# Two weight loads, the first reads of the way back and one first-stage result change queue and place, with four more filler matmuls

## The chip, the cores and the metric

The kernel runs on one core of one Trainium2 chip. The metric is the device time of one execution in microseconds, the median of several runs. The core has a matrix engine (PE, with its weight loads shown as PEld), a vector engine (DVE), an activation engine (ACT), a general engine (POOL) and a sync engine (SP). Each engine works through its own list of instructions in order. SP, ACT and POOL can also issue DMA transfers; a transfer that has to wait for something holds up all that stands behind it on the engine that issues it.

## The reference

```python
def _attn_ref(x, filt_r, filt_i):            # x: (8, 3008, 256)
    X = np.fft.rfft(x, axis=1)
    F = (filt_r + 1j * filt_i)[None, :, :]   # (1505, 256)
    y = np.fft.irfft(X * F, n=x.shape[1], axis=1)
    return y.astype(np.float32)

def _moe_ref(x, w_in, w_out):                # x: (24064, 256)
    h = x @ w_in                             # w_in: (256, 2048)
    g = h - np.tanh(h)
    return (g @ w_out).astype(np.float32)    # w_out: (2048, 256)
```

The first function filters eight sequences in the frequency domain, and the second is fed with its result, batch after batch, as 24064 rows. `x` and the filters come as float32. The two weight matrices come as 64-bit floats (their random values are scaled by a 64-bit factor), and the kernel converts them to 32 bits itself, with integer operations on their words.

## The kernel before, in words

The length 3008 is split as 64 x 47, so that each transform becomes two stages of matrix products. The first stage (`first`) multiplies the samples by a 64-point matrix for each of 47 residues; these are taken in pairs, which leaves 24 groups of rows. Its results are written to memory (`ct1`), read again in another order, taken through the 47-point stage (`forth`), multiplied by the filter (`filtered`) and taken back through the 47-point stage (`back`). The result goes to memory once more (`ct2`). The last stage (`last`, with the tile `e2` read from `ct2`) makes the rows `ut`, on which the two weight matrices work: `up` multiplies by `w_in`, `shrink` computes h - tanh(h) from a chain of activations, `down` multiplies by `w_out`. In most of the run `up` and `down` take seven products for eight, with seven planes of each weight matrix (`wu` and `wd`): planes 0, 1, 3 and 6 are converted weights, and planes 2, 4, 5 (and a new 6) are sums of them, made late by `sums`. For the first four units (`up_plain`, `down_plain`) only the four converted planes are used.

The first batch is handled in a prologue of its own, before any weight product runs. In it the 32 columns of the 47-point stage are cut in seven slots (`SLOTS`, six with five columns and one with two; `last_g` is 6). A loop over the slots `g` (L1264 to L1302) runs `forth`, `filtered` and the product back (`back0`, and `back` for the last slot), and `way_back()` (L1255) issues the product back of the slot that is next in line. `back0` writes its result to `ct2` through POOL's queue for the slots 0 to 2, SP's for 3 and 4, and ACT's for 5 (L1150). `back` for the last slot copies with ACT (L481) and writes each copy in two halves, one through ACT's queue and one through SP's (L483).

At the end of the prologue `rest(a, n, queues)` (L1130) reads the rows `a` to `a + n` of each of four groups from `ct2` into `e2`, in four DMAs (L1134): first the rows of the slots 0 to 4, as soon as they are written, and, after the last `way_back()`, the remaining seven. PE's first product of the main part (L595, in `last`) needs all of `e2`. Between these, `first(2, ...)` issues its first five loads from SP, `convert(100)` finishes the conversion of the first five pieces of weights, `first1` makes the first-stage results of the second batch that were not yet made (four matmul pairs, L1232, four ACT copies, L1238, and four writes to `ct1`, L1239), and `warmer(n)` issues `n` matmuls whose result nobody reads (L1086).

The weights come in 16 jobs of 512 KB. `begun` (L240) issues a job's raw load and returns a generator that then converts it in steps: an ACT activation (L181), five DVE operations (L183 to L194) and one or two DVE additions into `wu` or `wd` (L201). The first five jobs are converted in the prologue. The others go through `tiles1` (L1043), whose raw buffers are the halves of the tiles `ft` (two jobs), `a2` (two jobs), `ft` and so on, and whose working buffers are the halves of the tile `xy`, in turn. `buffer(tag)` (L278) gives the halves of a tile alternately. `weights` (L247) converts jobs 5 to 15 step by step in the first units of the main part, so that the place of each step in the engines' lists is fixed when the program is built, and issues the loads of the later jobs on POOL's queue.

The whole program is emitted with an order written out by hand: each engine executes in the order of the source, and only waits for data and buffers are put in automatically.

The lines that matter here: the loads of the jobs 7 and 8 (counted from 0) in the loop, L1281; the two calls of `rest`, L1303 and L1305; `convert(100)` and `first1`, L1308 and L1309; `warmer(8)`, L1314; the copies and writes of `first1`, L1234 to L1240.

Of the kernel before, what the change touches and what calls it, by code (L numbers as in the profile page):

```python
# [9 lines left out]
F32 = mybir.dt.float32  # L10
# [7 lines left out]
BATCH, SEQ, DM = 8, 3008, 256  # L18
NQ, NR = 64, 47
NA = NQ // 2  # L20
NH = (NR + 1) // 2
SG = 5
# [95 lines left out]
def kernel(  # L118
# [9 lines left out]
    nc = tc.nc  # L128
    V, G, ACT = nc.vector, nc.gpsimd, nc.scalar
    f_d, both_d, g_d, whole_d, mats_d, one_d, wide_d, pairs_d, whole_pairs_d, split_d = (  # L130
        nc.inline_tensor(v, name=n).ap()
        for v, n in zip(_consts(), ("f", "f_both", "g", "g_whole", "mats", "one", "wide",
                                    "g_pairs", "g_whole_pairs", "f_split")))

    ct1 = [nc.dram_tensor(f"ct1_{b}", (4 * NA * NH, DM), F32, kind="Internal")
           for b in range(1, BATCH)]
# [9 lines left out]
    def dram(t, off, dims):  # L146
        return bass.AP(tensor=t, offset=off, ap=[list(d) for d in dims])
# [20 lines left out]
    wu = cst.tile([128, 7, DFF // 2], F32, name="wu")  # L168
# [57 lines left out]
    def sums(u, n=4):  # L226

        w = (wu if u < 4 else wd)[:, :, 256 * (u % 4):256 * (u % 4) + 256]
        V.tensor_add(w[:, 4], w[:, 6], w[:, 3])
        yield  # L230
        for to, one_in, less in ((5, 4, 0), (2, 1, 5), (6, 0, 6))[:n - 1]:
            V.tensor_sub(w[:, to], w[:, one_in], w[:, less])
            yield
# [6 lines left out]
    def begun(tiles, job, queue=nc.sync):  # L240
        j = converted(tiles, *job, queue)
        next(j)
        return j
# [3 lines left out]
    def weights(tiles, jobs, queue, began, ahead, after=()):  # L247

        began += [begun(tiles, job, queue) for job in jobs[len(began):ahead]]
        yield  # L250
        for k in range(len(jobs)):
            pending[0] = len(jobs) - k
            for n, _ in enumerate(began[k]):
                yield
                if (after or k > 2) and n == 2 and k + 1 < len(jobs):
                    next(began[k + 1])
            if k + ahead < len(jobs):
                began.append(begun(tiles, jobs[k + ahead], queue))
            pending[0] = len(jobs) - k - 1
            for u in dict(after).get(k, ()):  # L260
                yield from sums(u)
# [16 lines left out]
    def buffer(tag):  # L278

        turns[tag] = 1 - turns.get(tag, 1)  # L280
        return kept[tag][:, turns[tag]]
# [755 lines left out]
    with tc.tile_pool(name="tr", bufs=2) as tr, tc.manual_schedule():  # L1037
# [16 lines left out]
        with tc.tile_pool(name="pro", bufs=1) as pro, \  # L1054
                tc.tile_pool(name="ps0", bufs=8, space=bass.MemoryType.PSUM) as ps0:

            def z0(name, shape):
                return ps0.tile(shape, F32, tag="z", bufs=8, name=name)
# [3 lines left out]
            def big(shape, dtype, name):  # L1062

                return pro.tile(shape, dtype, tag="big", bufs=3, name=name)
# [16 lines left out]
            def warmer(n, t=None):  # L1081

                warm = z0("warm", [128, 256])
                t = f0[:, 0:2].rearrange("p a n -> p (a n)") if t is None else t
                for _ in range(n):
                    nc.tensor.matmul(warm, t[:, 0:128], t, start=True, stop=True)  # L1086
# [43 lines left out]
            def rest(a, n, queues):  # L1130

                e2 = e2s[0][0]
                for j in range(4):
                    queues[j % len(queues)].dma_start(  # L1134
                        e2[NA * j + a:NA * j + a + n],
                        dram(ct2[0], (NA * j + a) * NH * DM, [[NH * DM, n], [1, CH * DM]]))
# [16 lines left out]
            last_g = len(SLOTS) - 1  # L1153
# [17 lines left out]
            jobs = parts_of((0, 1, 2, 4, 3, 5, 6, 7))  # L1171
# [5 lines left out]
            for c in range(3):  # L1177
# [14 lines left out]
                r = 8 * c  # L1192
# [27 lines left out]
            def convert(n):  # L1220

                for _ in range(n):
                    next(early, None)
# [3 lines left out]
            def first1(x1):  # L1227

                for r in range(0, 8, 2):
                    pf = z0("pf", [128, 2, DM])  # L1230
                    for k in range(2):
                        nc.tensor.matmul(pf[:, k], f0[:, r + k], x1[:, r + k],  # L1232
                                         start=True, stop=True)
                    if r % 4 == 0:  # L1234
                        two = (tr.tile([128, 2, 2, DM], F32, tag="a1", bufs=1, name="a1") if r else
                               buffer("xy").rearrange("p (m n) c -> p m n c", m=2))
                    a1 = two[:, r // 2 % 2]
                    ACT.copy(a1, pf)  # L1238
                    nc.sync.dma_start(  # L1239
                        dram(ct1[1], r * DM, [[NH * DM, 128], [1, 2 * DM]]), a1)  # L1240
                    yield

            a2 = {0: across(0)}
            convert(5)
# [19 lines left out]
            for g in range(last_g + 1):  # L1264
                if g == 2:
                    x1 = load_x(big([128, 8, DM], F32, "x1"), 1, 0, 8)
                if g + 2 <= last_g:
                    a2[g + 2] = across(g + 2)
                    if g + 2 < last_g:
                        fts[g + 2] = filters_of(g + 2)  # L1270
                        if g == 1:
                            fts[last_g] = filters_of(last_g)
                    else:
                        turned_in(fts[last_g])
                if g == 3:
                    under(fts[last_g])
                    e2s[0] = load_e2(0, 0, ())
                if g < last_g:
                    there[g + 1] = there0(g + 1)
                if g == last_g - 1:  # L1280
                    ahead += [begun(tiles1, job, queue=G) for job in jobs[7:9]]  # L1281
                    next(began[3])
                    way_back()
                next(there[g][0])
                if g < last_g - 2:
                    convert(3 if g < 3 else 1)
                xy = there.pop(g)[1]
                chain = filtered(g, xy, fts.pop(g), V, V if g in (0, last_g - 1, last_g) else G, pro)
                nn = next(chain)
                for _ in range(2):  # L1290
                    next(chain)
                if g in summed:
                    next(chain)
                ended.append((back, (0, g, xy, z0, (ACT, nc.sync))) if g in summed else (back0, (g, nn)))
                if g == 1:
                    next(turning)
                if g not in (0, last_g - 1):
                    way_back()
                if g == 2:
                    next(turning)  # L1300
                if g == 3:
                    ahead = [begun(tiles1, job, queue=G) for job in jobs[5:7]]  # L1302
            rest(0, SG * (last_g - 1), [nc.sync])  # L1303
            way_back()
            rest(SG * (last_g - 1), NA - SG * (last_g - 1), [nc.sync])  # L1305
            fs = first(2, z2, [(1, c) for c in range(2, NX)])
            next(fs)
            convert(100)  # L1308
            for _ in first1(x1):  # L1309
                pass  # L1310
            late = weights(tiles1, jobs[5:], G, ahead, 4,
                           after={6: (0,), 8: (1,), 10: (2, 4)})
            next(late)
            warmer(8)  # L1314

        with tc.tile_pool(name="dn", bufs=2) as dn, \
                tc.tile_pool(name="ps", bufs=1, space=bass.MemoryType.PSUM) as ps:
# [72 lines left out]
            for U in range(total + 2):  # L1390
# [8 lines left out]
                if U < total:  # L1399
                    p, c = groups[i]  # L1400
# [127 lines left out]
```

## Time and profile before

| | |
|---|---|
| median of three runs | 2541.26 us (2539.32 to 2542.22) |
| profiled execution | 2539.7 us |
| its span, first to last instruction | 2537.8 us |
| PE busy | 2522.2 us, 99% of the span |
| DVE, ACT, POOL busy | 76%, 67%, 60% |
| mean granted clock of PE | 0.998 |
| moved by DMA | 211.37 MB, 83 GB/s over the span |

The profile is of one execution. An engine's busy time counts its instructions, and a wait is put down to what ended last among the things waited for. In the chain of work that ended last, PE has 97% and DMA 2%. In the share of the DMA engines that is busy, the 40 equal slices of the span show 0.8, 0.8 and 0.6 of full in the first three, of 63 us each, and 0.4 or less after them, so transfers are dense only in the prologue and the first units after it. In rows of a timeline, a group such as "x4" stands for four instructions in a row, with the start of the first and the time to the end of the last.

### The profile page before, as it was taken

Reading aid. Unit: us, or ns where it says so; the run is one execution under the profiler, and the core shown is the slowest. Engines: PE = TensorE matmul, PEld = TensorE weight load, DVE = VectorE, ACT = ScalarE, POOL = GpSimd, SP = SyncE. Lnnn points to the kernel's source line nnn. Section 1 sums busy time; section 2 is a strip of 40 time slices with the busy share of each in tenths; the row PEclk is TensorE's granted clock in tenths of the full one; section 3 lists DMA queues with packets and bytes.
Section 4 is the critical chain, followed back from the end, with each engine's and each line's share of the span. In section 5 each row is a group of like instructions: output and inputs, shape, how many; then the busy total and the mean of one; then the engine's idle time right before and its main releaser. Section 6 shows DMA issues by size and latency. Waiting matters only on the chain.

```text
span 2537.8 us, 44568 instructions
## 1 busy us (share of the span) xinstructions
PE 2522.2 (99%) x17068; PEld 2173.2 (86%) x17068; DVE 1934.3 (76%) x2272; ACT 1694.0 (67%) x2552; POOL 1532.4 (60%) x1112
## 2 busy tenths in 40 slices
PE   9999999999999999999999999999999999999998
PEld 8678889888898888988888888888889888898887
DVE  6888877988688876888669886698866888555555
ACT  4666666667666766676667666666666666666665
POOL 4256666667566765676656665666655666455552
PEclk9999999999999999999999999999999999999999
DMA  8864223422343323342334322443123322110110
GB/s 247 260 161 106 71 50 101 111 69 52 87 104 94 80 72 86 82 111 59 82 85 108 88 53 71 97 115 84 36 72 84 92 66 53 26 31 19 25 23 19
DMA packets 333664, 211.37 MB, mean 83 GB/s; under 512 B 231645, under 2 KB 305531, under 8 KB 329793
## 3 DMA queue, kind: packets, MB, share of 16 engines
q1 hardware_dynamic: 319091, 184.93, 29.6%
q0 software_dynamic: 11120, 16.16, 2.2%
q10 hardware_dynamic: 3230, 7.34, 0.9%
q8 instruction: 136, 2.23, 0.4%
q14 instruction: 87, 0.71, 0.1%
HBM read 127.81 MB, written 83.39 MB: 83 GB/s over the span
## 4 chain that ended last, share of the span: by engine, by line
PE 97%; DMA 2%; DVE 1%; issue 0%; POOL 0%; SPq 0%; ACT 0%; POOLq 0%; DVEq 0%
PE o L826 44%; PE x L653 26%; PE z L653 13%; PE y L653 6%; PE pm L415 2%; PE pu L595 2%; PE o L888 1%; PE pm L351 1%; PE pf L308 1%; DMA filt<-in_filt_r_dram 1%; PE o L724 0%; DMA x<-in_x_dram 0%; PE x L724 0%; DMA ct<-e 0%; DMA filt_end<-filt 0%; PE z L724 0%
## 5 line engine op out<-in xcount | busy, mean ns | idle before, releaser
L826 PE MATMUL o<-t,wd 128*128 128x256 f32 (+1 forms) x3008 | 762.6, 376 | 0.0
L624 POOL TENSOR_TENSOR t<-h 128x512 f32<-128x512 f32 (+1 forms) x184 | 303.6, 1650 | 708.4 <-DVE h L776 642.1
L776 DVE TENSOR_TENSOR h<-h,y 128x1024 f32<-128x1024 f32 (+1 forms) x384 | 571.1, 1487 | 156.3 <-ACT y L772 156.3
L826 PEld LDWEIGHTS o<-t,wd 128*128 128x128 f32 x3008 | 568.8, 190 | 84.5 <-POOL o L858 15.1
L653 PE MATMUL x<-tu,wu 128*128 128x256 f32 (+1 forms) x2256 | 571.3, 376 | 0.0
L826 PE MATMUL o<-h,wd 128*128 128x256 f32 (+1 forms) x2256 | 569.9, 375 | 0.2 <-DVE h L776 0.2
L653 PEld LDWEIGHTS x<-tu,wu 128*128 128x128 f32 x2256 | 427.4, 190 | 53.8 <-issue 3.9
L826 PEld LDWEIGHTS o<-h,wd 128*128 128x128 f32 x2256 | 428.3, 190 | 50.9 <-issue 0.8
L659 ACT COPY s<-x 128x512 f32<-128x512 f32 (+1 forms) x188 | 109.3, 581 | 517.0 <-PE x L653 516.9
L769 ACT ACTIVATE y<-y 128x1024 f32<-128x1024 f32 (+1 forms) x384 | 399.5, 1040 | 12.1
L772 ACT ACTIVATE y<-y 128x1024 f32<-128x1024 f32 (+1 forms) x384 | 399.8, 1041 | 4.6
L766 ACT ACTIVATE y<-h 128x1024 f32<-128x1024 f32 (+1 forms) x384 | 400.6, 1043 | 2.5 <-DVE h L702 1.7
L627 POOL TENSOR_TENSOR t<-h,t 128x512 f32<-128x512 f32 (+1 forms) x184 | 338.3, 1839 | 0.0
L625 POOL TENSOR_TENSOR t<-h,t 128x512 f32<-128x512 f32 (+1 forms) x184 | 310.5, 1688 | 14.4
L626 POOL TENSOR_TENSOR t<-h 128x512 f32<-128x512 f32 (+1 forms) x184 | 277.0, 1506 | 0.0
L659 ACT COPY u<-x 128x512 f32<-128x512 f32 (+1 forms) x376 | 214.1, 569 | 71.8 <-PE x L653 69.1
L702 DVE COPY h<-x 128x512 f32<-128x512 f32 (+1 forms) x188 | 127.6, 679 | 129.0 <-PE x L653 128.8
L694 DVE TENSOR_TENSOR h<-z,u 128x512 f32<-128x512 f32 (+1 forms) x188 | 127.2, 677 | 87.8 <-ACT u L659 87.5
L653 PE MATMUL x<-ut,wu 128*128 128x256 f32 (+1 forms) x752 | 193.9, 380 | 0.0
L653 PE MATMUL y<-ut,wu 128*128 128x256 f32 (+1 forms) x752 | 190.1, 375 | 0.0
L653 PE MATMUL z<-ut,wu 128*128 128x256 f32 (+1 forms) x752 | 190.0, 375 | 0.0
L653 PE MATMUL z<-tu,wu 128*128 128x256 f32 (+1 forms) x752 | 190.0, 375 | 0.0
(218 smaller groups left out, 2933.8 us busy)
## 6 DMA issues: line engine op xcount, KB each, us to landing
ft<-filt SPq DMA_DIRECT2D x28, 1024.0 KB
ct<-nn SPq DMA_DIRECT2D x56, 512.0 KB
e<-ct SPq DMA_DIRECT2D x47, 512.0 KB
a<-ct SPq DMA_DIRECT2D x112, 192.0 KB
out_dram<-ot SPq DMA_DIRECT2D x1248, 16.0 KB
x_sb<-in_x_dram SPq DMA_DIRECT2D x110, 128.0 KB
ct<-a SPq DMA_DIRECT2D x60, 128.0 KB
ct<-x_sb SPq DMA_DIRECT2D x60, 128.0 KB
```

The source lines that it names most:

```text
L624: by.tensor_sub(t[0], b[0][1], b[0][0])
L625: by.tensor_sub(t[1], b[1][1], t[0])
L626: by.tensor_sub(t[2], b[1][1], b[0][1])
L627: by.tensor_sub(t[3], b[1][0], t[1])
L653: nc.tensor.matmul(bank[:, k], wu[:, q - 1, (2 * u + k) * 128:(2 * u + k + 1) * 128], rhs[q - 1], start=(first and k == 0), stop=True, ski ...
L659: ACT.copy(t, X)
L702: V.tensor_copy(h[:, 2, :, 0:w], X)
L766: ACT.activation(y[k], ht[k], AF.Arctan, scale=TURN)
L769: ACT.activation(y[k], y[k], AF.Tanh, scale=BEND)
L772: ACT.activation(y[k], y[k], AF.Square, scale=SCALE, accum_out=y_sums[:, 2 * U + k // 2:2 * U + k // 2 + 1])
L776: V.tensor_mul(ht[k], ht[k], y[k])
L826: nc.tensor.matmul(product(q), wd[:, q - 1, (2 * u + k) * 128: (2 * u + k + 1) * 128], rhs[q - 1][:, k], start=(u == 0 and k == 0 and q == ...
```

## The change

Five edits, all at the end of the prologue:

- The raw loads of the jobs 7 and 8 are no longer issued in the loop, from POOL, ahead of the last slots. Job 7 is issued after `convert(100)`, job 8 after `first1`, both from SP (the default queue of `begun`).
- The first four reads of `rest` (the rows of the slots 0 to 4) are issued from POOL instead of SP.
- `first1` copies its results into two planes of `wu` that hold nothing yet, plane 4 for the first two pairs and plane 5 for the others, in place of a half of `xy` and of a tile `a1`.
- It writes two of its results with one DMA, so that there are two DMAs of 512 KB in place of four of 256 KB.
- The filler has twelve matmuls in place of eight.

As `first1` no longer takes a half of `xy`, the conversions that follow begin with the other half.

```diff
@@ in first1 @@
                     for k in range(2):
                         nc.tensor.matmul(pf[:, k], f0[:, r + k], x1[:, r + k],
                                          start=True, stop=True)
-                    if r % 4 == 0:
-                        two = (tr.tile([128, 2, 2, DM], F32, tag="a1", bufs=1, name="a1") if r else
-                               buffer("xy").rearrange("p (m n) c -> p m n c", m=2))
-                    a1 = two[:, r // 2 % 2]
-                    ACT.copy(a1, pf)
-                    nc.sync.dma_start(
-                        dram(ct1[1], r * DM, [[NH * DM, 128], [1, 2 * DM]]), a1)
-                    yield
+                    two = wu[:, 4 if r < 4 else 5].rearrange("p (m n c) -> p m n c", m=2, n=2)
+                    ACT.copy(two[:, r // 2 % 2], pf)
+                    if r % 4:
+                        nc.sync.dma_start(
+                            dram(ct1[1], (r - 2) * DM, [[NH * DM, 128], [1, 4 * DM]]),
+                            two.rearrange("p m n c -> p (m n c)"))
+                        yield
@@ in the loop over the slots @@
                 if g == last_g - 1:
-                    ahead += [begun(tiles1, job, queue=G) for job in jobs[7:9]]
                     next(began[3])
                     way_back()
@@ after the loop @@
-            rest(0, SG * (last_g - 1), [nc.sync])
+            rest(0, SG * (last_g - 1), [G])
             way_back()
             rest(SG * (last_g - 1), NA - SG * (last_g - 1), [nc.sync])
             fs = first(2, z2, [(1, c) for c in range(2, NX)])
             next(fs)
             convert(100)
+            ahead.append(begun(tiles1, jobs[7]))
             for _ in first1(x1):
                 pass
+            ahead.append(begun(tiles1, jobs[8]))
             late = weights(tiles1, jobs[5:], G, ahead, 4,
                            after={6: (0,), 8: (1,), 10: (2, 4)})
             next(late)
-            warmer(8)
+            warmer(12)
```

## The prediction

> **What bounds the kernel now.** I read the page's first line, then TensorE's (PE's) waits, then the few microseconds in which there are any, engine by engine. The page:
>
> ```profile
> span 2537.8 us, 44568 instructions
> ```
>
> The profiled execution took 2539.7 us, 1.9 more than its span; the median of the three timed runs is 2541.26, 1.6 above it (they go from 2539.32 to 2542.22). The waits of PE from 82 us to the end of the span:
>
> ```profile
> PE pt L932 <- DVE o L858: 0.4, 1, 0.4
> PE o L826 <- DVE h L776: 0.2, 1, 0.2
> ```
>
> In 2455 us PE waits 0.6 us. Whatever happens ahead of 82 us is carried to the end one for one, and after it only a new wait can change the time. The change acts between 55 and 90 us, so PE's timeline there is what the sum is made from (columns: start, duration, work, and in brackets the idle time before it and what ended it):
>
> ```profile
> 65.87 1.10 PE L478 MATMUL pe<-xy,mats_sb 112*112 112x128 f32 x8 [0.37 <-DVE xy L458]
> 66.81 3.62 PE L1232 MATMUL pf<-x,f 128*128 128x256 f32 x16
> 70.26 3.62 PE L1086 MATMUL warm<-f 128*128 128x256 f32 x16
> 75.94 0.33 PE L595 MATMUL pu<-gt,e 64*64 64x64 f32 x4 [2.06 <-DMA e<-ct]
> 76.54 1.15 PE L595 MATMUL pu<-gt,e 64*64 64x64 f32 x60 [0.27 <-issue]
> 77.62 1.79 PE L1379 MATMUL pt<-mats_sb 120*120 120x256 f32 x4
> 79.20 2.74 PE L724 MATMUL x<-ut,wu 128*128 128x448 f32 x4
> 81.77 1.67 PE L724 MATMUL z<-ut,wu 128*128 128x448 f32 x4
> 83.28 3.17 PE L724 MATMUL o<-ut,wu 128*128 128x448 f32 x8
> ```
>
> Eight filler matmuls (L1086, two passes each) end at 73.88. Then PE idles 2.06 us until `e2`, the way back's result read again from memory, has landed, and 0.27 us more for its last piece. Four L724 matmuls take 1.51 us from 81.77 to 83.28, but 2.57 us from 79.20 to 81.77: there the clock was halved. Three stretches, with PE's busy time and the granted clock (the third number from the right):
>
> ```profile
> 38.00:41.50 3.50, 2.37 (x12) 1.70 (x11) 3.40 (x7) 0.59 (x1) 2.26 (x2) 1.00 0.40 100
> 74.56:77.97 3.41, 1.76 (x66) 1.58 (x67) 1.75 (x3) 0.20 (x1) 0.00 (x0) 1.00 0.67 199
> 77.97:81.38 3.41, 3.41 (x7) 1.89 (x6) 3.10 (x8) 1.02 (x3) 0.00 (x0) 0.50 1.03 244
> ```
>
> A stretch with PE 52% busy is followed by 3.41 us at half speed, which is 1.7 us of matmul work lost; an earlier one, 68% busy, is not. So up to 82 us there are two losses: the wait for `e2`, and the half-speed stretch behind it.
>
> **The change part by part.**
>
> *First reads of the way back, from SP's to POOL's queue (L1303).* SP's queue now, and what it waited for:
>
> ```profile
> 66.61 1.57 SPq L1134 DMA_DIRECT2D e<-ct  x4
> 69.98 0.82 SPq L483 DMA_DIRECT2D ct<-e  x2
> 73.18 1.03 SPq L1134 DMA_DIRECT2D e<-ct  x3
> ```
> ```profile
> SPq L483 <- DMA e<-ct: 1.7, 1, 1.7
> ```
>
> The last slot's results leave in halves, one on ACT's queue and one on SP's (L483), from the same copies:
>
> ```profile
> 66.57 0.37 ACT L481 COPY e<-pe 112x256 f32<-112x256 f32 x1 [0.44 <-PE pe L478]
> 66.97 0.33 ACTq L483 DMA_DIRECT2D ct<-e  x1
> 67.40 0.37 ACT L481 COPY e<-pe 112x256 f32<-112x256 f32 x1 [0.46 <-PE pe L478]
> 67.80 0.33 ACTq L483 DMA_DIRECT2D ct<-e  x1
> ```
>
> ACT's halves go 0.03 us after their copies. SP's have the four first reads ahead of them until 68.18 and then wait 1.7 us, by the trace for one of those reads to land; they go at 69.98, and 3.20 us later the last reads of `e2` can start (73.18). With the four reads gone from SP its halves go as ACT's do, at 67.0 and 67.8. From below: if they still wait for the reads, nothing is gained here. From above: 2.6 us, the second from about 70.4 to 67.8. I take 2.1, since the last reads also wait for ACT's write of 67.80, which needs the same 3.2 us: 71.0 to 71.1. PE saw `e2` 2.76 and, complete, 3.36 us after 73.18; after the change that is 73.9 and 74.5.
>
> The four reads themselves now pass through POOL's queue:
>
> ```profile
> 55.89 0.72 POOL L175 DMA_DIRECT2D a<-in_moe_w_out_dram  x1
> 59.16 0.72 POOL L175 DMA_DIRECT2D a<-in_moe_w_in_dram  x1 [2.54 <-DMA ft<-in_moe_w_in_dram]
> 82.72 0.72 POOL L175 DMA_DIRECT2D ft<-in_moe_w_in_dram  x1 [22.84 <-DVE xy L194]
> ```
> ```profile
> a<-in_moe_w_out_dram POOLq DMA_DIRECT2D x1, 512.0 KB, 6.6
> a<-in_moe_w_in_dram POOLq DMA_DIRECT2D x1, 512.0 KB, 6.0
> ct<-e POOLq DMA_DIRECT2D x2, 240.0 KB, 3.8
> ```
>
> They wait for the fourth slot group's writes as they do now, until 66.61, and nothing is queued behind them before 82.72, so POOL's wait holds up nobody. POOL needs 0.72 us for an issue where SP took about 0.4: the last starts at 66.61 + 3 x 0.72 = 68.8. Each moves 25 rows of 4 KB; the nearest row, 240 KB, takes 3.8 us, the farthest 6.6: landed at 72.6, at most 75.4. I take 72.6 to 73.5, ahead of the 74.5 of the last reads. Cost nothing; the cover is the last reads and the filler, and at the upper end it still just holds.
>
> *Four more filler matmuls (L1314).* Sixteen passes go from 70.26 to 73.88, some 0.217 us each; eight more are 1.7 us, and PE is free at 75.6. This is now later than `e2` (74.5), so PE passes to L595 without a gap. Of the 2.1 us won on `e2`, PE gets only 75.94 - 75.6 = 0.3 in its start, and 0.27 by the missing second wait. The gain that is left is the clock: the stretch up to 77.97 holds no gap above the few tenths that PE waits for `ut`, so it is far above 68% busy and I expect no half speed.
>
> The sum: L595 runs from 75.6 to 76.8 (60 of its pieces take 1.08 from 76.54 to 77.62). `ut` follows from it:
>
> ```profile
> 78.51 0.35 DVE L606 TENSOR_TENSOR ut<-pu,odd 128x192 f32<-128x192 f32 x1
> 78.78 0.41 DVE L605 TENSOR_TENSOR ut<-pu,odd 128x256 f32<-128x256 f32 x1
> 79.11 0.34 DVE L606 TENSOR_TENSOR ut<-pu,odd 128x192 f32<-128x192 f32 x1
> ```
>
> Its first half was done at 78.86, 1.17 us after L595's end (77.69), the second at 79.45. So 78.0 and 78.6 after the change; L724 starts at 78.1 (0.2 for its weights), does four in 1.51, and its second set starts at 79.6 instead of 81.77: 2.2 us earlier.
>
> *Two raw weight loads, from POOL's queue at 55.89 and 59.16 to SP's behind the last reads (after L1308 and L1309).* Ahead of 66 us 1 MB less is moved; DVE's wait for `filt_end` may shrink, and L478 may start up to its 0.37 us earlier, at best. I count 0.1. Behind, SP's queue:
>
> ```profile
> 74.58 0.35 SPq L295 DMA_DIRECT2D f<-f_both  x1
> ...
> 77.66 1.01 SPq L1239 DMA_DIRECT2D ct<-xy  x2
> ```
>
> The five loads of `first` take SP from 74.58 to 77.6, now from 72.5 to 75.5. There the first raw load is issued, then two stores of some 0.5 us, and the second raw load at about 77.1. ACT takes the loads up in its fixed order, as conversions of `a` (their starts are the last two numbers), and has a wait for a store among the conversions:
>
> ```profile
> L181 ACT ACTIVATE xy<-a x2: 673/678/683, 85.4 to 89.3; 128x512 f32<-128x512 f32 x2
> ...
> DMA ct<-xy: 4.4, 1
> ```
> ```profile
> 95.30 1.06 ACT L310 COPY a<-pf 128x512 f32<-128x512 f32 x2
> ```
> ```profile
> 97.25 1.03 PE L308 MATMUL pf<-x_sb,f 128*128 128x256 f32 x4
> ```
>
> Moved up 2.2 us with PE, the loads are needed at 83.2 and 87.1. Landing in 6.0 to 6.6 us as on POOL: 81.5 to 82.1, and 83.1 to 83.7. Both in time; cost nothing, lower bound nothing; the upper bound is a rival below. Behind an ACT that waits stand L727 and L310, and for L310 (done at 96.36) waits PE's third L308 at 97.25: only 0.89 us of slack.
>
> *Results of the second batch's first stage to two planes of `wu`, two stores in place of four (L1234).* The four copies stay. ACT's 4.4 us, in which a weight conversion waits for the store out of `xy`, go: the buffer is no longer in the way. PE does not wait for it today, so it counts zero; but DVE, which waits for ACT there, needs it to keep up with a PE that is 2.2 us earlier.
>
> Sum: 2.2 + 0.1 = 2.3 us, 2537.4 for the profiled execution, **2539.0** against the median; its own range is 2537.5 to 2540.5, from the 0.37 and the spread of the runs. That is 0.1%; a measurement tells about 0.2% (5.1 us) from no change.
>
> **The rivals.**
>
> *The half-speed stretch stays.* For it: the window at 77.97 may also count the small 64-wide matmuls of L595 as little work; against it, the 68% row. Then L724 starts at 78.1 at half speed and its second set comes at about 81.0: gain 0.8, 2540.5. The Trainium skill (TensorE: Matmul & The Clock Gate, section "What's actually happening") has the clock drop only after a whole idle window of about 3.4 us; by that rule a gap of 2.3 us is not the cause, and closing it would not help. The trace disagrees, with a drop behind a window in which PE was busy for 1.76 us; so the chance of this stays small.
>
> *The raw weights come late, and it ends slower.* Place: the two ACT conversions above. For it: the loads go from a time without consumers into the stretch with DMA share 1.03, behind five loads and, the second, two stores on the same queue. It begins to cost where the first takes over 7.7 us from issue or the second over 10.9 (87.1 + 0.9 - 77.1). From there each late microsecond is one of PE, and a gap of over 1.5 us brings another 1.7 us of half speed. Both 3.3 us late: -2.2 + 2 x (3.3 - 0.9) + 2 x 1.7 = +6.0, 2547. Against it: the store behind the same five loads, issued at 77.66, had landed before the conversion at 85.4, under 7.7 us, and the rows of the loads themselves say 6.0 to 6.6.
>
> *More than I count.* The timed runs' median is 1.6 above the profiled execution. If the gap costs them that much more, say by one further half-speed stretch of 1.7, the gain is 2.3 + 1.6 + 1.7 = 5.6: 2535.7. For it only that spread; against it that the profile shows no second stretch.
>
> **How the numbers follow.** The forecast gets 0.53, the half speed that stays 0.10, late weights 0.17 (0.13 of it over 0.2%), the larger gain 0.20 (0.18 of it over 0.2%). So faster 0.18, same 0.69, slower 0.13. Range 2535.8 to 2544.0: it takes in nearly all of the larger gain and the cheaper half of the late weights.
>
> **What would show it.** Right: L483 on SP at 67.0 and 67.8 with no wait for `e<-ct`; the last reads at 71; L1086 with 24 passes to 75.6 and L595 directly behind; granted clock 1.00 from 76 to 84; L724's second set at 79.6; no 4.4 at L181. Wrong: L595 still waiting for `e<-ct` (POOL's reads late); 0.50 anywhere; PE idle near 95 us, with ACT's L181 waiting for a raw load.

## The result, and the profile after

The changed kernel takes 2544.6 us (median of 22 runs) beside 2540.75 for the kernel before: 1.0016 times as long, with a 95% interval of 1.001 to 1.0022. That is 0.16% slower, a difference below the 0.2% that the prediction took as the limit, but with an interval clear of 1. The prediction had it 2.3 us faster (2539.0 beside the median of 2541.26 that it knew), with 2544.0 as its upper end.

The profiled execution took 2545.76 us, 6.06 more than the one before; its span is 2543.9 us, 6.1 more.

PE's waits from 82 us to the end (us in total, times, longest) have a new first row; the others are of 0.4 us and less, two of them as before and one new, of 0.2 us:

```profile
PE pf L308 <- DMA x_sb<-in_x_dram: 3.5, 1, 3.5
```

PE's timeline (start, duration, work, idle time before it):

```profile
66.26 1.10 PE L478 MATMUL pe<-xy,mats_sb 112*112 112x128 f32 x8 [0.52 <-DVE xy L458]
...
70.65 5.34 PE L1086 MATMUL warm<-f 128*128 128x256 f32 x24
76.09 1.38 PE L595 MATMUL pu<-gt,e 64*64 64x64 f32 x64
...
80.31 1.67 PE L724 MATMUL z<-ut,wu 128*128 128x448 f32 x4
...
94.29 1.67 PE L724 MATMUL x<-ut,wu 128*128 128x448 f32 x4
99.44 3.75 PE L308 MATMUL pf<-x_sb,f 128*128 128x256 f32 x8 [3.48 <-DMA x_sb<-in_x_dram]
102.98 2.87 PE L888 MATMUL o<-h,wd 128*128 128x448 f32 x4
105.69 1.67 PE L724 MATMUL z<-ut,wu 128*128 128x448 f32 x4
```

Up to 80 us it goes as planned: L595 follows the filler without a gap, and the second set of L724 (z) starts 1.46 us earlier than before (81.77). Then PE waits 3.48 us at its third L308, the first stage of the third batch, for that batch's samples; and behind the wait its matmuls take almost twice as long. The granted clock, third number from the right:

```profile
77.97:81.38 3.41, 3.23 (x10) 1.58 (x9) 3.27 (x9) 1.90 (x4) 0.00 (x0) 1.00 1.00 245
...
95.17:98.58 3.41, 0.78 (x3) 0.06 (x1) 1.04 (x3) 2.34 (x4) 0.71 (x1) 1.00 1.05 232
98.58:101.99 3.41, 2.55 (x6) 2.13 (x7) 3.34 (x6) 1.29 (x4) 0.00 (x0) 0.50 0.97 292
101.99:105.40 3.41, 3.41 (x7) 1.91 (x7) 2.80 (x6) 0.82 (x2) 0.71 (x1) 0.50 0.47 143
```

The half speed at 78 us is gone, and two such stretches stand at 98.58. PE is busy for 2.55 + 3.41 us in them and does half of that, so 2.98 us are lost. The balance of the two profiled executions: 1.46 won, 3.48 waited, 2.98 lost to the clock make +5.0 of the 6.1 us by which the span grew. The place agrees: at the last row above PE is 5.21 us behind the kernel before, whose same four products (z of L724) start at 100.48, and from about 200 us on it stays 5.8 behind, up to the last few microseconds. The other 1.1 us are not one wait; I leave them open.

The samples were issued in time. SP's queue, with the two raw weight loads (L175) and the samples of the third L308 (the last two rows):

```profile
67.35 1.20 SPq L483 DMA_DIRECT2D ct<-e  x2
71.88 1.43 SPq L1134 DMA_DIRECT2D e<-ct  x4
...
76.41 0.55 SPq L175 DMA_DIRECT2D a<-in_moe_w_out_dram  x1
77.06 0.88 SPq L1237 DMA_DIRECT2D ct<-wu  x2
78.04 0.74 SPq L175 DMA_DIRECT2D a<-in_moe_w_in_dram  x1
78.83 1.52 SPq L572 DMA_DIRECT2D gt<-g  x1
80.58 0.78 SPq L574 DMA_DIRECT2D e<-ct  x1
...
86.74 0.51 SPq L265 DMA_DIRECT2D x_sb<-in_x_dram  x1
87.30 0.61 SPq L271 DMA_DIRECT2D x_sb<-in_x_dram  x1
```

Before, the same samples went out later, and PE did not wait for them:

```profile
88.20 0.48 SPq L265 DMA_DIRECT2D x_sb<-in_x_dram  x1
88.72 0.62 SPq L271 DMA_DIRECT2D x_sb<-in_x_dram  x1
```

What differs is what they meet. The share of the 16 DMA engines that is busy (the number before the last) while the samples are issued, before and after:

```profile
85.50:88.50 3.00, 3.00 (x13) 2.20 (x12) 2.86 (x7) 1.99 (x5) 0.72 (x1) 1.00 0.73 283
```
```profile
85.50:88.50 3.00, 3.00 (x12) 1.94 (x11) 2.86 (x7) 1.72 (x4) 0.74 (x1) 1.00 1.03 405
```

Before, the engines had run out of work there for a while; after, they have not. What was moved toward that stretch are the two raw loads (512 KB each), which went at 55.89 and 59.16 and now go at 76.41 and 78.04; whether they are the reason is what the experiments try.

### The profile page after: what moved, and what is told of

Read it like the earlier page. It is cut to its first block, busy times and chain, and to the rows that moved or that the text cites. A ratio compares the mean times of both kernels' runs of the same rounds, so it can differ in the third digit from the quotient of the medians.

```text
span 2543.9 us, 44585 instructions
## 1 busy us (share of the span) xinstructions
PE 2526.1 (99%) x17076; PEld 2175.4 (86%) x17076; DVE 1936.3 (76%) x2272; ACT 1693.9 (67%) x2552; POOL 1531.9 (60%) x1114
## 3 DMA queue, kind: packets, MB, share of 16 engines
q8 instruction: 136, 2.23, 0.4%
## 4 chain that ended last, share of the span: by engine, by line
PE 94%; DMA 2%; DVE 2%; issue 1%; POOL 0%; ACT 0%; SPq 0%; ACTq 0%; DVEq 0%; POOLq 0%
PE o L826 44%; PE x L653 25%; PE z L653 12%; PE y L653 6%; PE pm L415 2%; PE pu L595 2%; PE pm L351 1%; DMA ct<-a 1%; DMA fh<-f 0%; DMA mats_sb<-mats 0%; DMA a<-in_moe_w_out_dram 0%; PE pf L308 0%; DMA filt<-in_filt_r_dram 0%; PE o L888 0%; DMA filt_end<-filt 0%
## 5 line engine op out<-in xcount | busy, mean ns | idle before, releaser
L653 PE MATMUL x<-tu,wu 128*128 128x256 f32 (+1 forms) x2256 | 571.4, 376 | 0.0
L653 PEld LDWEIGHTS x<-tu,wu 128*128 128x128 f32 x2256 | 427.3, 190 | 54.0 <-issue 4.2
L653 PE MATMUL x<-ut,wu 128*128 128x256 f32 (+1 forms) x752 | 194.0, 380 | 0.2 <-DVE h L702 0.2
L653 PE MATMUL y<-ut,wu 128*128 128x256 f32 (+1 forms) x752 | 190.1, 375 | 0.0
L653 PE MATMUL z<-tu,wu 128*128 128x256 f32 (+1 forms) x752 | 190.0, 375 | 0.0
L653 PE MATMUL z<-ut,wu 128*128 128x256 f32 (+1 forms) x752 | 190.0, 375 | 0.0
```

What stands on the lines that cost most here:

```text
L653: nc.tensor.matmul(bank[:, k], wu[:, q - 1, (2 * u + k) * 128:(2 * u + k + 1) * 128], rhs[q - 1], start=(first and k == 0), stop=True, ski ...
```

## The experiments

The first theory: 1 MB more in the stretch from 76 us, in which the DMA engines are busy all the time anyway, leaves a backlog when the third L308's samples are issued; PE waits for them and the clock doubles the damage. Its first rival: PE, 1.5 us earlier by the other edits, simply runs ahead of its samples, and the raw loads have nothing to do with it. A second rival came later: not the time of the raw loads counts but that they stand ahead of the samples in SP's queue. Last, each of the other edits is tried alone.

All medians are of 11 or 12 runs (8 in e11), all ratios against the runs of the kernel before on the same chip, with 95% intervals. The experiments ran on three chips, on which the median of the kernel before was 2541.02 us (e1 to e4), 2541.12 (e5 to e8) and 2540.3 (e9 to e12), so ratios are compared below rather than medians. Each trace is of one execution.

### e1: the two raw loads back in the loop, on POOL

```diff
 # changed kernel
+                    ahead += [begun(tiles1, job, queue=G) for job in jobs[7:9]]
-            ahead.append(begun(tiles1, jobs[7]))
-            ahead.append(begun(tiles1, jobs[8]))
```

> The changed kernel with one part undone: the raw loads of the jobs 7 and 8 are issued from POOL in the loop again. Theory 1 (their 1 MB, moved into the stretch in which the DMA engines are full, makes the samples for the third L308 late): PE's wait of 3.5 us at the third L308 and the 6.8 us of half speed go, the 1.5 us won up to 82 us stay: about 2539, 0.05 to 0.1% faster than the kernel before. Theory 2 (a PE that is 1.5 us earlier runs ahead of transfers that do not come earlier): the wait stays, about 2544.

Measured: 2539.55 us, ratio 0.9996 (0.9986 to 1.0006), clear of the 1.0016 (1.001 to 1.0022) of the whole change.

```profile
80.21 1.67 PE L724 MATMUL z<-ut,wu 128*128 128x448 f32 x4
...
96.55 1.97 PE L308 MATMUL pf<-x_sb,f 128*128 128x256 f32 x8 [0.69 <-DMA x_sb<-in_x_dram]
```

All that the other edits won is kept up to 80 us, and the wait at the third L308 shrinks from 3.48 to 0.69 us with no half speed behind it. The rival accounts for those 0.69 us at most.

### e2: the kernel before, with the two raw loads alone moved

```diff
 # kernel before
-                    ahead += [begun(tiles1, job, queue=G) for job in jobs[7:9]]
             convert(100)
+            ahead.append(begun(tiles1, jobs[7]))
             for _ in first1(x1):
                 pass
+            ahead.append(begun(tiles1, jobs[8]))
```

> The kernel before with only the two raw loads moved to SP, behind the last reads. Theory 1: the wait at the third L308 appears, shorter by some 1.5 us since PE is that much later, with half speed behind it; 2543 to 2547. Theory 2: PE is no earlier, so no wait; 2541, as before.

Measured: 2544.1 us, ratio 1.0007 (0.9997 to 1.0017).

```profile
75.28 0.33 PE L595 MATMUL pu<-gt,e 64*64 64x64 f32 x4 [0.47 <-DMA e<-ct]
...
101.42 3.75 PE L308 MATMUL pf<-x_sb,f 128*128 128x256 f32 x8 [5.93 <-ACT xy L181]
```
```profile
99.08 1.07 ACT L310 COPY a<-pf 128x512 f32<-128x512 f32 x2 [1.72 <-DMA ct<-a]
```
```profile
91.24 0.68 ACT L181 ACTIVATE xy<-a 128x512 f32<-128x512 f32 x1 [2.25 <-DMA a<-in_moe_w_in_dram]
```

The move alone brings the wait, 5.93 us of it in this execution; by the time of its runs e2 is not told apart from no change. ACT is named as what ended the wait, but the samples' last share landed 0.14 us before PE started (the table below). The samples are not the only thing that is late here. ACT waits 2.25 us for the second raw load and 1.72 us for a store of its own (`ct<-a`), so its copies out of `pf`, which the third L308 overwrites, run from 99.08 to 100.15. PE could not have begun before the first of them had ended, at about 99.7: with the samples in time some 4.2 of the 5.93 us would have been left. After the whole change the same copies start at 95.76, and of its 3.48 us they explain no more than 0.5.

### e3: the changed kernel with eight fillers

```diff
-            warmer(12)
+            warmer(8)
```

> The changed kernel with eight filler matmuls. The reads of e2 had all landed at about 75.2 us of the changed kernel's trace, and the filler ended at 76.1: L595 starts 0.9 us earlier, behind a gap of about 1 us. If that gap brings half speed, 1 to 1.5 us are lost there. Theory 1 and 2 both: the samples for the third L308 come at their own time, so the wait there takes up what is won; about the time of the changed kernel, within 1.5 us.

Measured: 2542.51 us, ratio 1.0008 (0.9999 to 1.0017).

```profile
76.28 1.47 PE L595 MATMUL pu<-gt,e 64*64 64x64 f32 x64
...
98.94 1.97 PE L308 MATMUL pf<-x_sb,f 128*128 128x256 f32 x8 [2.18 <-ACT y L772]
```

With the raw loads late the third L308 waits with eight fillers too. In this execution L478 began at 68.17, 1.91 us later than after the whole change, so `e2` was there when eight fillers ended; it says nothing of what the four fillers are worth.

### e4: the raw loads at their new place in the program, but on POOL

```diff
-            ahead.append(begun(tiles1, jobs[7]))
+            ahead.append(begun(tiles1, jobs[7], queue=G))
 ...
-            ahead.append(begun(tiles1, jobs[8]))
+            ahead.append(begun(tiles1, jobs[8], queue=G))
```

> The changed kernel with the two raw loads at their new place in the order, but issued from POOL, which reaches them at about 68 us, some 8 us ahead of SP. Theory 1: much of their 1 MB moves ahead of the full stretch, in the calm one of 70 to 76 us; the wait at the third L308 shrinks to under 1 us; e2 may land up to 1 us later; about 2539 to 2541. Theory 3 (what counts is that they stand ahead of the samples in SP's queue): no wait either. Theory 2: the wait stays, 2544.

Measured: 2540.57 us, ratio 1.0000 (0.9991 to 1.0008). POOL has nothing else to do there and issues them at 67.10 and 67.90:

```profile
96.03 1.89 PE L308 MATMUL pf<-x_sb,f 128*128 128x256 f32 x8
```

No wait, no half speed. But queue and time had changed together, which e10 and e11 take apart.

### e5: other bytes out of the way of the samples

The changed kernel; the 640 KB for group 1 of the main loop are issued behind the samples.

```diff
-                    if i + 1 < len(groups) and u == (2 if (p, c) == (0, NC - 1) else 0):
+                    if i + 1 < len(groups) and u == (1 if U < 4 else 2 if (p, c) == (0, NC - 1) else 0):
```

> The changed kernel with one edit: the 640 KB that group 1 needs only at about 125 us (gt and e2, L572 and L574, issued by SP at 78.8 and 80.6) are issued behind the samples of the third L308 (87.3). The two raw loads stay on SP where the change put them. Theory (too many bytes ahead of the samples in the full stretch from 76 us, whichever bytes they are): PE's wait at the third L308 falls from 3.5 to under 1.8 us (640 KB at the 380 GB/s of that stretch are 1.7 us), ACT's wait at 95.8 for ct<-a falls as well, the 6.8 us at half speed go or halve, 2541 us or less, some 3 below the changed kernel. Rival (the place of the raw loads matters by itself, as the conversions follow them in order): the wait stays at 3 us or more and the time within 1 us of the changed kernel's.

Measured: 2542.84 us, ratio 1.0007 (0.9998 to 1.0016).

```profile
95.40 1.89 PE L308 MATMUL pf<-x_sb,f 128*128 128x256 f32 x8
...
113.12 1.02 PE L888 MATMUL o<-h,wd 128*128 128x448 f32 x2 [1.33 <-DVE wd L201]
```

Half right. The wait at the third L308 is gone altogether, by moving other bytes than the raw loads, which speaks for the amount ahead of the samples as what makes it. The time falls by less than the 3 us expected, though: its interval meets both that of the whole change and 1. And PE has a new wait 18 us further on, for a weight matrix whose conversion is late. That the bytes now behind the samples are what made it late was not tried.

### e6, e7, e9: each of the other edits alone, on the kernel before

```diff
 # e6
-            warmer(8)
+            warmer(12)
 # e7
-            rest(0, SG * (last_g - 1), [nc.sync])
+            rest(0, SG * (last_g - 1), [G])
 # e9: first1 as in the changed kernel
+                    two = wu[:, 4 if r < 4 else 5].rearrange("p (m n c) -> p m n c", m=2, n=2)
 ...
```

> The kernel before with 12 fillers in place of 8 and nothing else. Fillers end at about 75.6, e2 comes at about 75.9 as before: L595 starts at 76.1 to 76.4 with a wait of 0.6 us or less. If the waits of 2.06 and 0.27 us ahead of L595 are what brings the stretch at half speed (0.50 from 77.97), it goes, and the second set of L724 (z) starts at 80.3 to 80.6 rather than 81.77, 1.2 to 1.5 us earlier: 2539.3 to 2539.8 beside 2540.8, less 0.7 given back at the third L308 as in e1 where PE runs ahead. Rival: the half speed has another cause and stays, z at 81.8 or later, no gain.

> The kernel before with the four first reads on POOL and nothing else. Eight fillers end at 73.9; the last reads start at 71 rather than 73.2, so e2 is there at 74.5 to 75.2 and L595 waits 0.6 to 1.3 us rather than 2.3. If the half speed needs a longer pause than that, z starts at 79.4 to 80.1 and the time is 1.5 us or more below before, less what the third L308 gives back; if it stays, z starts at 80.7 and the time is about 1 us below before.

> The kernel before with the second batch's first-stage results through the weights' unused planes and two stores, and nothing else. ACT's wait of 4.4 us for the store out of xy goes, no PE wait stood behind it: within 0.5 us of before, 2540.5 to 2541.5, L595 still waits for e2 by about 2 us and the half speed behind it stays. A gain of 1 us or more would mean that the wait of ACT had cost PE time further on.

Measured: e6 2540.59 us, ratio 1.0002 (0.9993 to 1.0011); e7 2539.79 us, 0.9998 (0.9987 to 1.0009); e9 2539.83 us, 0.9999 (0.9990 to 1.0007). In the timelines of PE, e6:

```profile
75.23 0.33 PE L595 MATMUL pu<-gt,e 64*64 64x64 f32 x4 [0.68 <-DMA e<-ct]
...
79.81 1.67 PE L724 MATMUL z<-ut,wu 128*128 128x448 f32 x4
...
95.30 1.99 PE L308 MATMUL pf<-x_sb,f 128*128 128x256 f32 x8
```

e7:

```profile
74.73 0.33 PE L595 MATMUL pu<-gt,e 64*64 64x64 f32 x4 [1.07 <-DMA e<-ct]
75.55 1.15 PE L595 MATMUL pu<-gt,e 64*64 64x64 f32 x60 [0.49 <-DMA e<-ct]
...
79.54 1.67 PE L724 MATMUL z<-ut,wu 128*128 128x448 f32 x4
...
95.02 1.89 PE L308 MATMUL pf<-x_sb,f 128*128 128x256 f32 x8
```

and e9:

```profile
75.96 0.33 PE L595 MATMUL pu<-gt,e 64*64 64x64 f32 x4 [2.60 <-DMA e<-ct]
...
79.14 2.83 PE L724 MATMUL x<-ut,wu 128*128 128x448 f32 x4
81.80 1.67 PE L724 MATMUL z<-ut,wu 128*128 128x448 f32 x4
```

The fillers alone and the earlier reads alone each end the half speed and bring z to 79.81 and 79.54 in these executions (before: 81.77). The way through `wu` alone changes nothing there: the wait, the half speed (2.83 us for the four matmuls) and z at 81.80 stay. In e6 and e7 PE is earlier than in the changed kernel, and its third L308 does not wait: the rival that PE outruns its samples falls as the cause of the 3.48 us. None of the three can be told from the kernel before by its time.

Their traces show something else. The 2 us that e6 and e7 have won do not reach the end. A product of L653, which starts at 141.86 in the kernel before, waits in e6:

```profile
141.86 1.03 PE L653 MATMUL x<-ut,wu 128*128 128x256 f32 x4
```
```profile
141.97 1.13 PE L653 MATMUL x<-ut,wu 128*128 128x256 f32 x4 [0.60 <-DVE h L702]
```

In e6 the 1.96 us at z are gone there, and in e7, where it starts at 142.14, the 2.23 us. Both have PE waits of a few tenths between 127 and 142 us, for ACT and DVE, which the kernel before has not. Nor is it these two alone: e4 wins 1.22 us at z and starts that product at 142.14. e10 keeps its 0.99 us to the end.

### e8: a version without the loss, with less filler

The changed kernel with the raw loads back as in e1, `warmer(10)`, and the edit of e5.

> The changed kernel with the two raw loads back on POOL in the loop, ten fillers in place of twelve, and gt and e2 of group 1 behind the samples of the third L308. Fillers end at 74.8, e2 comes at 74.5 to 75.1: L595 at 74.8 to 75.3, z at 79.2 to 79.6, some 2.2 to 2.5 us earlier than before and 0.7 to 1 earlier than e1. By the theory of too many bytes the third L308 waits for under 0.7 us, and the time is 2538.3 to 2539.2. By its rival (PE simply runs ahead of its samples, whatever is in front of them) everything won beyond e1 is given back at the third L308, which waits 1.4 us or more, and the time is e1's, 2539.6.

Measured: 2540.02 us, ratio 0.9999 (0.9990 to 1.0008).

```profile
95.93 1.89 PE L308 MATMUL pf<-x_sb,f 128*128 128x256 f32 x8
```

The third L308 does not wait, against the rival; the gain over e1 did not come: L478 began 1.12 us later here than in e1 (67.26 for 66.14). No version in this study is faster than the kernel before by more than its interval.

### e10 and e11: queue and time apart

```diff
 # e10: on SP, early
             rest(0, SG * (last_g - 1), [G])
             way_back()
+            ahead.append(begun(tiles1, jobs[7]))
+            ahead.append(begun(tiles1, jobs[8]))
             rest(SG * (last_g - 1), NA - SG * (last_g - 1), [nc.sync])
 # e11: on POOL, held back until e2 has landed
+            held = cst.tile([128, 1], F32, name="held")
+            G.tensor_copy(held[96:128], e2s[0][0][96:128, 0, 0:1])
+            ahead.append(begun(tiles1, jobs[7], queue=G))
+            ahead.append(begun(tiles1, jobs[8], queue=G))
```

> The changed kernel with the two raw loads still on SP, but ahead of the last reads of e2 (issued at 68 to 70 us, where the stretch 70 to 76 has a DMA share of 0.46) and not behind the samples at 76 and 78. If the time of issue decides: no long wait at the third L308, no half speed behind it, the time of the kernels with the loads off the full stretch, 2539.5 to 2541 (e2 may come up to 1 us later, as in e4). If SP's queue decides: as the changed kernel, 2543 or more, with a wait of 2 us or more near 95 to 100 us.

> The changed kernel with the two raw loads on POOL, held there by a copy of a column of e2 until e2 has landed, so that POOL issues them at 75.5 to 77.5 as SP does in the changed kernel. With e4 (POOL, 67 us) and e10 (SP, 69 us) it makes the square of queue and time. If the time of issue decides: as the changed kernel, 2542.5 to 2545, PE waits 2 us or more between 88 and 115 us or a raw load holds up ACT or DVE there. If SP's queue decides (the raw loads stand ahead of the samples in it): 2541 or less, no such wait.

Measured: e10 2540.87 us, ratio 1.0005 (0.9996 to 1.0013); e11 2547.16 us, ratio 1.0029 (1.0018 to 1.0039). In e10 the loads go out on SP at 69.17 and 69.68. PE waits 1.19 us for `e2` at L595, and not at its third L308:

```profile
96.26 1.89 PE L308 MATMUL pf<-x_sb,f 128*128 128x256 f32 x8
```

In e11, on POOL's timeline and on PE's:

```profile
74.50 0.75 POOL L175 DMA_DIRECT2D a<-in_moe_w_out_dram  x1
75.24 0.74 POOL L175 DMA_DIRECT2D a<-in_moe_w_in_dram  x1
```
```profile
98.48 3.38 PE L308 MATMUL pf<-x_sb,f 128*128 128x256 f32 x8 [3.45 <-DMA x_sb<-in_x_dram]
```

That fills the square of queue and time of issue:

```
          issued at 67 to 70 us          issued from 74.5 us on
POOL      e4   2540.57, 1.0000           e11   2547.16, 1.0029
SP        e10  2540.87, 1.0005           after 2544.6,  1.0016
```

On POOL the time of issue makes a difference by intervals that do not meet. On SP they meet narrowly, and there it is the wait that tells them apart. Between the queues no difference shows at either time. So the time of issue decides, as far as this tells. The Trainium skill (DMA: Bandwidth & Descriptors, section "Issuing engines are not separate DMA queues") says that transfers issued from any engine end up on the same 16 DMA engines and mix there; this square agrees. Why e11's ratio lies above that of the whole change, if it does (the intervals meet), is open: its profiled execution (2542.78 us) is the fastest of its eight, and it has a copy on POOL that the others have not.

### e12: one of the two loads back

```diff
+                    ahead += [begun(tiles1, job, queue=G) for job in jobs[7:8]]
-            ahead.append(begun(tiles1, jobs[7]))
```

> The changed kernel with the first of the two raw loads back in the loop on POOL, the second left on SP at its new place. 512 KB rather than 1 MB go into the full stretch. If the bytes decide, the time lies between those with none and with both there: 2540.5 to 2543, PE's wait near 95 us at 0.7 to 2.5 us. If the lateness of the first load itself decides (ACT's L181 in order): as with both back, 2539.5 to 2540.5.

Measured: 2541.74 us, ratio 1.0002 (0.9993 to 1.0011), between none (e1) and both (after), with an interval that meets both of theirs:

```profile
97.88 3.53 PE L308 MATMUL pf<-x_sb,f 128*128 128x256 f32 x8 [2.31 <-ACT y L772]
```

The wait is smaller with half the bytes, 2.31 us rather than 3.48, as the first theory has it, in one execution of each.

### All together

For every kernel: median and ratio, and from the profiled execution the DMA share from 85.5 to 88.5 us, the landing of the last share of the third L308's samples (us, as counted in the last section), and PE's wait there.

```
                               median  ratio   DMA share  landed   wait us
before                        2540.75            0.73      95.44    0
e9  first1 alone              2539.83  0.9999    0.84      94.56    0
e6  fillers alone             2540.59  1.0002    0.85      91.68    0
e7  reads alone               2539.79  0.9998    0.83      94.77    0
e1  raws back                 2539.55  0.9996    0.85      96.41    0.69
e4  raws on POOL, 67 us       2540.57  1.0000    0.82      95.09    0
e8  raws back, group 1 later  2540.02  0.9999    0.47      94.20    0
e10 raws on SP, 69 us         2540.87  1.0005    0.60      94.51    0
e12 one raw late              2541.74  1.0002    1.04      97.74    2.31
e3  raws late, 8 fillers      2542.51  1.0008    1.04      98.85    2.18
e5  raws late, group 1 later  2542.84  1.0007    1.03      94.75    0 (1.33 later)
e2  raws late alone           2544.1   1.0007    1.03     101.28    5.93
after                         2544.6   1.0016    1.03      99.35    3.48
e11 raws late, on POOL        2547.16  1.0029    1.03      98.34    3.45
```

In the eight kernels whose raw loads go before 70 us the DMA engines have free time when the samples are issued; in the six with one or two loads from 74.5 us on they have none, and five of these six get their samples later than all eight. The sixth, e5, has fewer bytes ahead of them. By ratio the six are slower than the eight (0.9996 to 1.0005) except for e12, but only after and e11 are clear of no change. A wait is that of one execution, in e3, e10 and e11 of the fastest one, and is not the whole of a median.

## Why the prediction was wrong

**The step that failed** is the one on the two raw loads: "Both in time; cost nothing, lower bound nothing". As far as it went it was nearly true. By their completion events the loads landed 6.87 and 9.89 us after their issue, where 6.0 to 6.6 had been taken; ACT waited for no more than one of them, and by 0.68 us:

```profile
88.01 0.69 ACT L181 ACTIVATE xy<-a 128x512 f32<-128x512 f32 x1 [0.68 <-DMA a<-in_moe_w_in_dram]
```

But it asked only whether the moved loads come in time, and not what they push back. The row with the DMA share of 1.03 stood in the prediction; what 1 MB more in such a stretch would delay was not asked. It delayed the samples of the third L308, which the step does not mention: issued 1.4 us earlier than before, they were complete 3.91 us later (99.35 for 95.44), and PE waited 3.48 us and then ran at half speed, which cost 2.98.

**The rival "the raw weights come late"** had the loss in the right place (near 95 us) and of the right kind (a wait of PE and then half speed). That its +6.0 us are so near the 6.06 us of the profiled execution is luck: it added up two late conversions of 3.3 us each, and between the medians there are 3.85 us. Its victim and its condition were wrong. It named the two conversions on ACT, to begin to cost from 7.7 and 10.9 us after issue; the second started 9.97 us after it, the 0.68 us of waiting included, and PE's wait came from elsewhere. Nor did its condition for half speed, a gap of over 1.5 us, hold each time: e3 waits 2.18 us and has none. Its chance of 0.17 rested on landing times of 6.0 and 6.6 us. They had been measured in a stretch that was as full (share 0.95 from 55.9 to 62.5, 1.00 from 59.16 to 65.2), and yet the second load took 9.89 us at its new place (share 1.02), so the share alone does not size a landing.

**First reads to POOL: right.** SP's halves of L483 went at 67.35 with L478 0.39 us later than before; in SP's waits none for `e<-ct` is left at L483:

```profile
SPq L483 <- ACT e L481: 4.4, 2, 4.0
```

The last reads started at 71.88 (forecast 71.0 to 71.1). e7 has the effect alone; since the half speed is gone there with eight fillers, no run shows what four more add to it.

**Four more fillers: as forecast.** L1086 has 24 passes and L595 follows without a gap; z is at 80.31 where 79.6 was forecast, 0.49 of it because L478 itself began at 66.26 rather than 65.77. Over the fourteen profiled executions L478 begins between 64.87 (e6) and 68.17 (e3), so the 0.1 us counted for that start was far below what it varies by:

```profile
64.87 1.04 PE L478 MATMUL pe<-xy,mats_sb 112*112 112x128 f32 x8
```
```profile
68.17 1.10 PE L478 MATMUL pe<-xy,mats_sb 112*112 112x128 f32 x8 [0.51 <-DVE xy L458]
```

**Half speed at 78 us: gone, as forecast**, so that rival fell: the granted clock is 1.00 from 77.97 to 81.38. The Trainium skill's rule (TensorE: Matmul & The Clock Gate, section "What's actually happening") that the clock falls after a whole idle window of about 3.4 us would have left it there; e6 and e7, which each only shorten the gap of 2.06 us, agree with the trace and not with that rule. The 52% and 68% of the prediction are not two sides of a threshold, though: in e3 a stretch with PE busy for 45% was followed by no half speed (below).

**Results through `wu`: right**, zero. ACT's 4.4 us for the store are gone, and e9 finds no difference.

**The sum** of 2.3 us was sized on a single execution, and it carried what is won up to 82 us to the end "one for one". That failed too: in e6 and e7 about 2 us are won at z and none is left at 142 us, where PE waits for DVE. The same edits without the raw loads' move (e1) came out at 2539.55, ratio 0.9996 with 0.9986 to 1.0006: near the forecast of 2539.0, but not told apart from no change. In its trace 1.56 us are won at z, and after the 0.69 us at the third L308 and later waits the span is 0.6 us shorter than before. So in these traces the forecast 2.3 us are not there without the moved loads either, though e1's interval does not exclude them.

## What to carry to other kernels

A load that is moved into a stretch whose DMA share is near 1 can cost something even if it is itself nearly in time: look for the next transfer in that stretch with a consumer on the bounding engine, and ask whether the DMA engines still run dry before it is issued. Another queue did not help here. An issue ahead of an emptier stretch did: in e4 and e10 the loads go just before the one from 70 to 76 us, where the share was 0.31 in the kernel before, and in e1 they go some 10 us before it. A wait of PE of 2 us or more is to be priced with the half speed that may follow it. And what PE wins early has to be followed to the next place where another engine is just in time for it, here 60 us further on.

## What the runs showed of the hardware

**The last share of a transfer can be several microseconds behind the others.** The trace has 16 completion events for each of these transfers. For the second half of the third L308's samples, counted from those events (us):

```
         shares done by     last share    PE's third L308 starts
before   16 by 95.44        95.44         97.25, no wait
e1       15 by 94.02        96.41         96.55
e12      14 by 94.60        97.74         97.88
e11      14 by 94.03        98.34         98.48
e3       13 by 95.54        98.85         98.94
after    13 by 96.05        99.35         99.44
e2       15 by 94.81        101.28        101.42
```

In each of the six kernels with a wait PE starts 0.09 to 0.14 us after the last share, also where the row names ACT as what ended it. Thirteen to fifteen shares are there by 94 to 96 us, nearly in time; the wait is for the one to three that are behind, in e2 by 6.5 us. A mean share of 1.03 does not show this; the events do not name the engine, so which engines lag, and why, was not measured. The Trainium skill (DMA: Bandwidth & Descriptors, section "Why a DMA increments its semaphore by 16 and not by 1") says that a transfer runs on up to 16 DMA engines that finish independently and that only the full count means it has landed; these events agree, as PE never starts before the sixteenth.

**Half speed needs no wholly idle stretch, and its length differs.** A stretch of 3.41 us with PE busy for 0.78 of it was followed by 6.83 us at half speed, though PE was busy for 2.55 us, 75%, of the first half of these. Waits of 3.45 us in e11 and 2.31 us in e12 were each followed by 3.41 us of it, and one of 2.18 us in e3 by none. Nor does PE's busy share alone decide: the 3.41 us from 74.53 in the kernel before, with PE busy for 1.73, were followed by half speed, and those from 95.23 in e3, with 1.53, were not. Where the wait falls in the sequence of such stretches may matter; I did not test that.

**That the loads at 56 and 59 us had cost the way back time is not shown.** In e2, without them there, the wait for `e2` ahead of L595 was 0.47 us rather than 2.06. But 0.93 of these 1.59 us come from the filler, which ends later because L478 started later (66.80 for 65.87), and 0.66 from an earlier `e2`; in e6, with the loads at their old place, L595 starts as early (75.23 for 75.28).
